# Cosine attention and an MLP mixer on one core: three row tiles of the sixth batch leave the slots and join the end's block products

## The chip, the core and the metric

One core of a Trainium2 chip runs the whole program. The metric is device time in microseconds (us) of one execution, as the median of the runs shown. The profile is of one other execution, whose span runs from its first to its last instruction. Engines are named as in the profile: PE (TensorE), DVE (VectorE), ACT (ScalarE), POOL (GpSimd), and SP, which here only issues DMAs. Each engine works through its own instructions in the order of the program, and waits where an operand or a buffer is not ready.

## The reference

```python
q, k, v: (8, 12, 448, 64)                      # batches, heads, rows, width; tau = 0.1
q_n = q / (norm(q) + 1e-6);  k_n = k / (norm(k) + 1e-6)
attn = softmax(q_n @ k_n.T / tau)
x = (attn @ v).transpose(0, 2, 1, 3).reshape(8, 448, 768)
h = relu(x.transpose(0, 2, 1) @ w_tok1) @ w_tok2      # 448 -> 256 -> 448, along the rows
u = x + h.transpose(0, 2, 1)
out = u + relu(u @ w_ch1) @ w_ch2                      # 768 -> 1536 -> 768, along the columns
```

Operands of the matrix products are fp16, sums and outputs fp32. In the code the hidden values `relu(u @ w_ch1)` are `gts`, and `u` is kept in `u16`, with its transpose in `ut`. The batches are numbered 0 to 7, so the sixth batch is number 5 in the code.

## The kernel before

**Slots.** A pair is two heads of one batch: 6 pairs to a batch, 48 in all. The loop at L920 runs one slot for each pair `i` from 7 to 47, and the program is written out by hand in the order in which each engine is to take it. A slot's own work is a software pipeline:

- PE: the scores of pair i (`score`, L345, three of them and the remainder, L352), weights times v for pair i-1 (`pv_rest`, `pv`, L367 and L384), and the token products of pairs i-2 (`tok2`, L434) and i-1 (`tok1`, L420).
- ACT: the exponentials (L346, L353), and the two steps of the norms of pair i+2 (L277, L278).
- DVE: the sums of squares of pair i+3 (L266, at the end of the slot), the last steps of the norms (L274, L275), and the evictions `rec`, `x`, `rt` and `u`.
- POOL, in `side(i)`: a cast of v of pair i (L228, and L230 in every third slot), the squares of pair i+3 (L250), and the scaling of k and q of pair i+2 into `kq` (L298, L306).
- SP: `tpose_dma(i + 2)` (L330) transposes that `kq` into `qk` by DMA, and the scores of slot i+2 read it. Behind it on the same queue come the loads of later pairs, the output stores, and `udma` (L443), which transposes `u`.

**Channel units.** The two channel products are cut into units: a G unit is one of 12 column tiles of `w_ch1` for a batch (`m_ch1`, 6 matmuls of 448 columns, L467), an F unit is one half of a row tile of the output (`m_ch2`, 12 matmuls of 384 columns, L483, with an addition of `u` on DVE and a store). They stand in `queue`. In each slot `fed[0]` grows by `fed[1]`. One unit is issued after `pv`, and more after `tok2` while `due()` says so. `refill(b)` queues a batch's units and sets `fed[1]` to their sum over six slots. A batch of 448 rows is three row tiles of 128 rows and one of 64, and the last 64 rows of an even batch share a tile (number 3 of the odd batch) with the first 64 of the next.

**The end.** Batches 6 and 7 (`B0`, `B1`) do not go through units. After the last slot their channel products are done as 2 by 2 block products with 7 block multiplications in place of 8 (the sums and differences of operands are made by `fast_weights1`, `fast_weights2`, `fast_x` and `fast_g`). The first channel product is `p1` to `p7` (L587). The second is `q1` to `q7` (`prod2`, L675): seven products of 6 matmuls of 384 columns for each pair of row tiles in `TILES`. Three pairs are done so, and the shared tile of batches 6 and 7 by plain matmuls (`shared_half`, L743). In their blocks the recorded line of DVE's and POOL's additions is that of the helper `tt`, L536, so the prediction names them by tile.

Weights for the block products are prepared inside the last slots. In POOL's order: `fast_weights2(1)` (`t1w`) in slot 41, ahead of that slot's scaling; `fast_weights2(2)` (`t2w`) in slots 45 and 46; `fast_weights1(1)` (`s1w`) after that; and `fast_weights1(4)` (`s4w`) after slot 47's cast. DVE makes `s2w` from `s1w` in slot 47, right after the evictions of `pv` of pair 46:

```python
            if i == NP_ALL - 2:
                fast_weights2(2, (1,))
                fast_weights1(1, nc.gpsimd)
```

PE's PSUM buffers with the tag "b" are two. In slot 47 and just after it they are used in turn by `psO` of pair 46 (two), `psU` of pair 45, `psR` of pair 46, and `psO` of pair 47 (two), so that PE's `pv_rest` of pair 47 waits until DVE has evicted `psR` of pair 46 (`rt`).

Of the kernel before, what the change touches and what calls it, by code (L numbers as in the profile page):

```python
# [22 lines left out]
def kernel(  # L23
# [12 lines left out]
    nc = tc.nc  # L36
# [479 lines left out]
    def ch2_units(b):  # L516
        cuts = ((0, DH, None), (DH, D, 0))
        ends = ((0, DH, None), (DH, D - 128, 0), (D - 128, D, D - 128))
        if b == B - 1:
            order = [(m, c) for m in (3, 0, 1, 2) for c in (ends if m == 2 else cuts)]  # L520
        elif b == 0:
            order = [(m, c) for c in cuts for m in range(3)]
        else:
            order = [(m, c) for m in range(3) for c in cuts]
            if b % 2:
                order[5:5] = [(3, cuts[0])]
                order.append((3, cuts[1]))
        return [(ns(hi - lo, CT), lambda wide, m=m, lo=lo, hi=hi, st=st: m_ch2(b, m, lo, hi, st, wide))
                for m, (lo, hi, st) in order]

    HD, HC = DT // 2, CT // 2
    B0, B1 = B - 2, B - 1
    fw = {}

    def tt(eng, out, a, b, op):
        eng.tensor_tensor(out=out, in0=a, in1=b, op=op)  # L536
# [4 lines left out]
    def tail_tiles():  # L541
        fw["t"] = {k: xtile(k, "x", [128, HD, S]) for k in (1, 2)}
        fw["e1"] = tail.tile([128, 2, S], FP32, name="e1_0", tag="e1")
        fw["s"] = [tail.tile([128, HD, C // 2], FP16, name=f"s{n}w1") for n in (1, 2, 4)]

    def xtile(k, name, shape):
        return (tail if k < 3 else tail2).tile(shape, FP16, name=f"t{k}{name}", tag=f"t{k}x", bufs=1)
# [47 lines left out]
    def gpart(i, b, d):  # L595
        return gts[B0 // 2][:, HC * i + 2 * d:HC * i + 2 * d + 2, b * S:(b + 1) * S]

# [28 lines left out]
    def p4(d):  # L626
        prod1(4, d, py, False)
        tt(nc.vector, gpart(1, 0, d), py[d][:, :, 0:S], e["e1", d][:], ALU.add)
# [21 lines left out]

    TILES = ((0, 1), (2, 6), (4, 5))
    ENDS = ((0, 256), (256, DH))
    sg, xo, yo, zo, eo, orow = {}, {}, {}, {}, {}, {}

    def gtile(t, i, j0=0, j1=HC):
        return gts[B0 // 2][:, HC * i + j0:HC * i + j1, 128 * t:128 * t + 128]

    def fast_g(g, k, j0=0, j1=HC):
        if k == 1 and j0 == 0:
            sg[g] = {n: tail2.tile([128, HC, 128], FP16, name=f"s{n}g_{g}", tag=f"s{n}g", bufs=1) if g == 1  # L660
                     else xtile(n, f"g_{g}", [128, HC, 128]) for n in (1, 2, 3, 4)}
        r1, r2 = TILES[g]
        s = sg[g]
        a, b, op = {1: (gtile(r2, 0, j0, j1), gtile(r2, 1, j0, j1), ALU.add),
                    2: (s[1][:, j0:j1], gtile(r1, 0, j0, j1), ALU.subtract),
                    3: (gtile(r1, 0, j0, j1), gtile(r2, 0, j0, j1), ALU.subtract),
                    4: (gtile(r1, 1, j0, j1), s[2][:, j0:j1], ALU.subtract)}[k]
        tt(nc.vector, s[k][:, j0:j1], a, b, op)

# [8 lines left out]
    def j3(ap):  # L678
        return ap.rearrange("p (j e) -> p j e", e=128)

    def urow(t, h):
        b, slot = (B0, t) if t < 3 else (B1, t - 3)
        return u16[b][:, HD * h:HD * (h + 1), slot]

    def etile2(kind, g, bufs=2):
        eo[kind, g] = tail2.tile([128, DH], FP32, name=f"{kind}_{g}", tag=kind.replace("f", "e") if kind in ("f5", "f16", "f167") else kind, bufs=bufs)
        return eo[kind, g][:]

# [7 lines left out]
    def f1u(g):  # L696
        tt(nc.gpsimd, j3(etile2("f1u", g, 1)), j3(eo["f1", g][:]), urow(TILES[g][1], 0), ALU.add)

    def q5(g):
        zo[g], yo[g] = [ps2.tile([128, 512], FP32, name=f"ps{a}o_{g}", tag="s") for a in "ZY"]  # L700
        prod2(5, g, zo[g], True)
        nc.scalar.activation(out=etile2("f5", g), in_=zo[g][:, 0:DH], func=AF.Copy)

    def q6(g):
        prod2(6, g, yo[g], True)
        tt(nc.vector, etile2("f16", g), yo[g][:, 0:DH], eo["f1", g][:], ALU.add)
        tt(nc.gpsimd, j3(eo["f16", g][:]), j3(eo["f16", g][:]), urow(TILES[g][0], 1), ALU.add)
        tt(nc.gpsimd, j3(eo["f5", g][:]), j3(eo["f5", g][:]), urow(TILES[g][1], 1), ALU.add)

# [7 lines left out]
    def q7(g):  # L717
        prod2(7, g, yo[g], False)
        tt(nc.vector, etile2("f167", g), yo[g][:, 0:DH], eo["f1", g][:], ALU.add)
        tt(nc.gpsimd, orow[g][1][:, DH:D], eo["f167", g][:], eo["f5", g][:], ALU.add)  # L720

    def store_row(t, o, lo=0, hi=D, first=nc.sync):
        b, m = (B0, t) if t < 3 else (B1, t - 4)
        r = 0
        for n, (c, p0, p1_) in enumerate(pieces(*MAIN[m])):
            eng = nc.sync if n else first
            eng.dma_start(out=out[b].rearrange("(p c) d -> c p d", c=NCH)[c, p0:p1_, lo:hi], in_=o[r:r + p1_ - p0, lo:hi])
            r += p1_ - p0

    def q3(g):  # L730
        prod2(3, g, zo[g], False)
        tt(nc.vector, orow[g][0][:, DH:D], zo[g][:, 0:DH], eo["f16", g][:], ALU.add)

    def q4(g):
        prod2(4, g, yo[g], False)
        tt(nc.vector, orow[g][1][:, 0:DH], yo[g][:, 0:DH], eo["f1u", g][:], ALU.add)
        store_row(TILES[g][1], orow[g][1])

    def shared_half(h):
        lo = DH * h  # L740
        psF = ps2.tile([128, 512], FP32, name=f"psF_shared_{h}", tag="s")
        for ct in range(CT):
            nc.tensor.matmul(psF[:, 0:DH], gts[B0 // 2][:, ct, 384:512], wc2t[:, ct, lo:lo + DH],  # L743
                             start=(ct == 0), stop=(ct == CT - 1))
        o = qkv.tile([128, DH], FP32, name=f"ost_shared_{h}", tag=("qf", "kf")[h])
        (c, p0, p1_), = pieces(384, S)
        for r, b, slot in ((0, B0, 3), (64, B1, 0)):
            tt(nc.vector, j3(o[r:r + 64]), j3(psF[r:r + 64, 0:DH]), u16[b][r:r + 64, HD * h:HD * (h + 1), slot], ALU.add)
        for r, b in ((0, B0), (64, B1)):
            nc.sync.dma_start(out=out[b].rearrange("(p c) d -> c p d", c=NCH)[c, p0:p1_, lo:lo + DH], in_=o[r:r + 64])  # L750

# [11 lines left out]

    KEPT = 6000.0

    def refill(b):
        new = ch1_units(b) + ch2_units(b)
        segs = NPAIR + 1 if b == 0 else NPAIR
        fed[1] = (sum(t for t, _ in new) - (KEPT if b == 0 else 0.0)) / segs
        queue.extend(new)  # L770

    with tc.manual_schedule():
# [147 lines left out]
        for i in range(NPAIR + 1, NP_ALL):  # L920
# [20 lines left out]
            elif pj == 2 and 1 < b < B - 1:  # L941
                refill(b - 1)
            side(i)
            if i == NP_ALL - NPAIR:
                fed[1] = (sum(t for t, _ in queue) - fed[0]) / NPAIR
# [17 lines left out]
            if i == NP_ALL - 3:  # L963
                early.close()
                tail = ctx.enter_context(tc.tile_pool(name="tail", bufs=1, side="right", reuse_waits="tile"))
                tail_tiles()
            if i == NP_ALL - 2:
                fast_weights2(2, (1,))
                fast_weights1(1, nc.gpsimd)
# [3 lines left out]
        while queue:  # L973
            unit(True)
        gts[B0 // 2] = mix.tile([128, CT, 2 * S], FP16, name=f"gt_{B0 // 2}", tag="gt", bufs=1)
        p1(0)
# [5 lines left out]
        for k in (3, 4):  # L982
            fw["t"][k] = xtile(k, "x", [128, HD, S])
        fast_weights1(3, nc.vector)
        p1(1)
# [33 lines left out]
        p6(2)  # L1019
        p4(0)  # L1020
        relu(1, 0, 0)
        p4(1)
        relu(1, 0, 1)
        p7(2)
        bank2("Z", 1)
        p5(1)
# [4 lines left out]
        p4(2)  # L1031
        relu(1, 0, 2)
        p3(1)
        fast_g(0, 1)
        fast_g(0, 2)
        p3(2)
        q1(0)
        f1u(0)
        relu(0, 1, 1)
        fast_g(0, 3)  # L1040
        q1(1)
        relu(1, 1, 1)
        q5(0)
        relu(0, 1, 2)
        relu(1, 1, 2)
        q6(0)
        fast_g(0, 4)
        for g in range(2):
            rows(g)
            q2(g)  # L1050
            fast_g(g + 1, 1)
            q7(g)
            fast_g(g + 1, 2)
            q3(g)
            store_row(TILES[g][0], orow[g][0])
            fast_g(g + 1, 3)
            q4(g)
            fast_g(g + 1, 4)
            if g == 0:
                f1u(1)  # L1060
            else:
                q1(2, ENDS)
                f1u(2)
            q5(g + 1)
            q6(g + 1)
        rows(2)
        q3(2)
        store_row(TILES[2][0], orow[2][0], DH, D)
        q7(2)
        shared_half(0)  # L1070
        q4(2)
        shared_half(1)
        for (lo, hi), eng in zip(ENDS, (nc.sync, nc.scalar)):
            q2(2, lo, hi)
            store_row(TILES[2][0], orow[2][0], lo, hi, eng)

# [34 lines left out]
```

## Time and profile before

| | |
|---|---|
| median of 3 runs | 383.1 us (382.84 to 383.28) |
| the profiled execution | 380.6 us, span 378.8 us |
| busy in the span | PE 366.2, POOL 286.9, DVE 246.0, ACT 234.0 us |
| granted TensorE clock | 1.00 |
| PE between 60 and 310 us | no idle time |
| last matmul starts its group at | 372.55 us |

The busy time of an engine is the union of its instructions. Matmuls overlap each other, so a group's own length is read from the start of one group to the start of the next: an F unit takes 1.95 us so, a G unit 1.135 us, a product of the second block stage 0.975 us.

### The profile page before, as it was taken

The numbers are of one execution on the slowest core, as the hardware profiler recorded it, in microseconds if no ns is written. First come the engines' busy times: TensorE is split into PE (matmuls) and PEld (weight loads), VectorE is DVE, ScalarE is ACT, GpSimd is POOL, SyncE is SP. The second block draws the span as 40 slices with busy tenths as digits, with TensorE's granted clock in tenths as the row PEclk, the third lists the DMA queues.
The fourth block names the chain that finished last, engine by engine and source line by source line (L and its number), as shares of the span: only waits on it lengthen the run. The fifth ranks groups of instructions, "written<-read, shape, count | busy, mean of one in ns | idle before, by whom it ended". The sixth has DMA issues, their size and how long they took to land.

```text
span 378.8 us, 10270 instructions
## 1 busy us (share of the span) xinstructions
PE 366.2 (97%) x4086; PEld 240.1 (63%) x4086; DVE 246.0 (65%) x559; ACT 234.0 (62%) x401; POOL 286.9 (76%) x414
## 2 busy tenths in 40 slices
PE   7788999999999999999999999999999999999994
PEld 6466666676567666667656666666666667655562
DVE  7789766777436574557444675456545776887963
ACT  5999887855666447855675466764677574426410
POOL 8999997979667577678657757767869987389760
PEclk9999999999999999999999999999999999999999
DMA  8999999989997898969895798977984874200144
GB/s 225 281 231 218 262 239 200 207 159 157 217 220 141 180 201 209 187 167 170 213 210 121 175 184 198 195 162 197 205 192 104 158 160 99 57 0 3 55 123 116
DMA packets 116256, 64.35 MB, mean 170 GB/s; under 512 B 72304, under 2 KB 112880, under 8 KB 116208
## 3 DMA queue, kind: packets, MB, share of 16 engines
q1 hardware_dynamic: 110208, 58.20, 69.9%
q0 software_dynamic: 5616, 5.21, 8.7%
q8 instruction: 32, 0.52, 0.6%
q10 hardware_dynamic: 384, 0.29, 0.2%
q14 instruction: 16, 0.13, 0.1%
HBM read 43.45 MB, written 11.01 MB: 144 GB/s over the span
## 4 chain that ended last, share of the span: by engine, by line
PE 81%; DMA 7%; DVE 4%; POOL 3%; ACT 1%; issue 1%; SPq 0%; DVEq 0%; POOLq 0%
PE psG L467 21%; PE psF L483 19%; PE psO L384 9%; PE psS L345 7%; PE psU L434 5%; PE psR L420 5%; DMA qf<-in_q_dram 3%; PE psY L587 3%; PE psYo L675 2%; DMA kf<-in_k_dram 2%; PE psX L587 2%; PE psQ L352 2%; POOL kq L298 2%; PE psZ L587 2%; PE psZo L675 1%; DVE ssq L266 1%
## 5 line engine op out<-in xcount | busy, mean ns | idle before, releaser
L346 ACT ACTIVATE pt<-psS 128x896 f16<-128x896 f32 (+1 forms) x156 | 132.7, 916 | 51.9 <-PE psS L345 51.9
L483 PE MATMUL psF<-wc2t,gt 128*128 128x384 f16 x504 | 88.4, 326 | 0.0
L467 PE MATMUL psG<-ut,wc1t 128*128 128x448 f16 x432 | 88.1, 352 | 0.0
L298 POOL TENSOR_TENSOR kq<-kf,rn 128x384 f16<-128x384 f32 (+1 forms) x47 | 41.9, 891 | 59.2 <-DVE rn L275 55.6
L483 PEld LDWEIGHTS <-gt 128*128 128x128 f16 x504 | 47.1, 98 | 27.8
L467 PEld LDWEIGHTS <-wc1t 128*128 128x128 f16 x432 | 40.2, 98 | 32.4
L470 ACT ACTIVATE gt<-psG 128x448 f16<-128x448 f32 x72 | 38.9, 540 | 33.1 <-PE psG L467 33.1
L266 DVE TENSOR_REDUCE ssq<-sq 128x15 f32<-128x960 f32 (+2 forms) x51 | 56.2, 1101 | 2.9 <-ACT sq L248 1.8
L423 DVE TENSOR_SCALAR rt<-psR 128x256 f16<-128x256 f32 x48 | 20.1, 418 | 50.8 <-PE psR L420 50.8
L298 POOL TENSOR_TENSOR kq<-qf,rn 112x512 f16<-112x512 f32 x45 | 47.0, 1045 | 3.0
L345 PE MATMUL psS<-qk 64*128 64x448 f16 x312 | 41.3, 355 | 3.5 <-DVE qk L324 2.8
L487 DVE TENSOR_TENSOR ost<-psF,u 128x384 f32<-128x384 f32 (+1 forms) x48 | 25.7, 536 | 26.8 <-PE psF L483 25.4
L250 POOL TENSOR_TENSOR sq<-qf 112x512 f32<-112x512 f32 x39 | 40.6, 1040 | 0.0
L250 POOL TENSOR_TENSOR sq<-kf 128x384 f32<-128x384 f32 (+1 forms) x46 | 40.2, 873 | 0.3 <-DMA kf<-in_k_dram 0.3
L384 PE MATMUL psO<-vt,pt 128*128 128x65 f16 (+1 forms) x1024 | 39.2, 193 | 0.0
L388 DVE TENSOR_TENSOR x<-psO,rec 128x256 f16<-128x256 f32 x82 | 34.8, 425 | 2.8
L384 PEld LDWEIGHTS <-pt 128*128 128x128 f16 (+1 forms) x1024 | 34.2, 97 | 3.5 <-issue 0.9
L437 DVE TENSOR_TENSOR u<-psU,x 128x512 f16<-128x512 f32 x48 | 32.3, 674 | 2.0 <-PE psU L434 0.5
L434 PEld LDWEIGHTS <-w2t 128*128 128x128 f16 x384 | 24.8, 98 | 7.9 <-issue 1.0
L420 PEld LDWEIGHTS <-w1t 128*128 128x128 f16 x384 | 24.8, 98 | 7.9 <-issue 2.1
L434 PE MATMUL psU<-rt,w2t 128*128 128x128 f16 x384 | 29.3, 219 | 0.5 <-POOL w2t L198 0.5
L420 PE MATMUL psR<-x,w1t 128*128 128x128 f16 x384 | 29.3, 219 | 0.2 <-DVE u L437 0.2
(128 smaller groups left out, 481.0 us busy)
## 6 DMA issues: line engine op xcount, KB each, us to landing
qf<-in_q_dram SPq DMA_DIRECT2D x47, 224.0 KB, 4.2
kf<-in_k_dram SPq DMA_DIRECT2D x36, 192.0 KB, 3.9
vf<-in_v_dram SPq DMA_DIRECT2D x36, 192.0 KB, 3.8
vf<-in_v_dram SPq DMA_DIRECT2D x12, 224.0 KB, 7.6
kf<-in_k_dram SPq DMA_DIRECT2D x11, 224.0 KB, 7.2
wc1t<-in_moe_w_ch_dram POOLq DMA_DIRECT2D x4, 576.0 KB, 10.1
wc2t<-in_moe_w_ch_dram POOLq DMA_DIRECT2D x2, 1152.0 KB, 11.8
out_dram<-ost SPq DMA_DIRECT2D x6, 336.0 KB, 3.6
```

Of the source, the lines that this page charges most:

```text
L250: nc.gpsimd.tensor_mul(out=dst, in0=src, in1=src)
L266: nc.vector.tensor_reduce(out=st["ssq"][0:n, sl], in_=st["sq"][0:n, sl], axis=AXX.X, op=ALU.add)
L298: eng.tensor_tensor(out=kq[0:p, a, 0:n].rearrange("p c g e -> p g c e"), in0=st["kq"[a]][:].rearrange("p (g c) e -> p g c e", g=2), in1=_b ...
L345: nc.tensor.matmul(psS[:, hh, 0:S], qk[hb, c * n:c * n + 128], qm[hb], start=True, stop=True)
L346: nc.scalar.activation(out=pts[i % 2][0:n, 2 * S * c:2 * S * (c + 1)].rearrange("p (h s) -> p h s", h=2), in_=psS[0:n, :, 0:S], func=AF.Ex ...
L384: nc.tensor.matmul(psO[:, m, 0:E + 1], pts[i % 2][0:n, at:at + 128], vt[0:n, i % HP, nch * hh + c, 0:E + 1], start=(old(i) and c == 0), st ...
L388: nc.vector.tensor_tensor(out=st["x"][:, :, hh * E:(hh + 1) * E], in0=psO[:, :, 0:E], in1=_bcast_free(rec[:], E), op=ALU.mult)
L420: nc.tensor.matmul(psR[:, tt], w1t[:, w1[m], tt * 128:(tt + 1) * 128], st["x"][:, m], start=(m == 0), stop=(m == 3))
L434: nc.tensor.matmul(psU[:, m], w2t[:, tt, lo:lo + 128], st["rt"][:, tt], start=(tt == 0), stop=(tt == TT - 1))
L467: nc.tensor.matmul(psG[:, 0:S], wc1t[:, dt, ct * 128:(ct + 1) * 128], ut[b][:, dt].rearrange("p m s -> p (m s)")[:, lo:lo + S], start=(dt ...
L470: nc.scalar.activation(out=gt[:, ct, (b % 2) * S:(b % 2 + 1) * S], in_=psG[:, 0:S], func=AF.Relu)
L483: nc.tensor.matmul(psF[:, 0:hi - lo], gt[:, ct, at:at + 128], wc2t[:, ct, lo:hi], start=(ct == 0), stop=(ct == CT - 1))
```

## The change

Three row tiles of batch 5 (`KEPT_B` in the diff; its tiles 0, 1 and 2; six F units) are no longer issued as units. Only the tile that batches 4 and 5 share remains (two F units, in slots 46 and 47). The end's second channel product works on ten row tiles in five pairs (`n` in the diff), where it had six in three pairs and one by plain matmuls: tiles 7, 8 and 9 are those of batch 5, and tile 3 is the shared one of batches 6 and 7. `shared_half` is gone. Batch 5's hidden values stay in their buffer, and batch 6's are written beside them, in the place of batch 4's. Batch 7's go into a new tile, with two small DMAs that bring batch 6's last 64 rows beside them (`g_shared`) and one for `u` (`u_shared`). The first pair's operands are made in part in slot 46: two `fast_g` on DVE, at the slot's end. The feed of channel work is no longer set anew at each `refill`, but is 4350 from slot 14 and 3400 from slot 38. From slot 42 it is, as before, a sixth of what is left.

Where the units land, in slots 36 to 47 (F b.m is tile m of batch b, a and b its halves; the bar is where the second place in the slot begins):

| slot | before | after |
|---|---|---|
| 36 | G4.10, G4.11, F4.0a | G4.5 to G4.8 |
| 37 | F4.0b, F4.1a | G4.9 to G4.11, F4.0a |
| 38 | F4.1b, F4.2a | F4.0b |
| 39 | F4.2b, G5.0 to G5.2 | F4.1a, F4.1b |
| 40 | G5.3 to G5.7 | F4.2a, F4.2b |
| 41 | G5.8 to G5.11 | G5.0 to G5.2 |
| 42 | F5.0a | G5.3, G5.4 |
| 43 | F5.0b, F5.1a | G5.5, G5.6 |
| 44 | F5.1b | G5.7, G5.8 |
| 45 | F5.2a | G5.9, G5.10 |
| 46 | F5.3a, F5.2b | G5.11, F5.3a |
| 47 | F5.3b | F5.3b |

```diff
     def ch2_units(b):
...
+            if b == KEPT_B:
+                order = [(3, c) for c in cuts]
...
-    TILES = ((0, 1), (2, 6), (4, 5))
+    TILES = ((7, 8), (0, 1), (2, 9), (4, 5), (6, 3))
...
+    RATES = {2 * NPAIR + 2: 4350.0, NP_ALL - 10: 3400.0}
     def refill(b):
         new = ch1_units(b) + ch2_units(b)
-        segs = NPAIR + 1 if b == 0 else NPAIR
-        fed[1] = (sum(t for t, _ in new) - (KEPT if b == 0 else 0.0)) / segs
+        if b == 0:
+            fed[1] = (sum(t for t, _ in new) - KEPT) / (NPAIR + 1)
         queue.extend(new)
...
             side(i)
+            fed[1] = RATES.get(i, fed[1])
             if i == NP_ALL - NPAIR:
                 fed[1] = (sum(t for t, _ in queue) - fed[0]) / NPAIR
...
             if i == NP_ALL - 2:
+                fast_g(0, 1)
+                fast_g(0, 2)
                 fast_weights2(2, (1,))
                 fast_weights1(1, nc.gpsimd)
...
         p7(2)
+        fast_g(0, 3)
+        fast_g(0, 4)
         bank2("Z", 1)
...
-        rows(2)
-        q3(2)
-        store_row(TILES[2][0], orow[2][0], DH, D)
-        q7(2)
-        shared_half(0)
-        q4(2)
-        shared_half(1)
-        for (lo, hi), eng in zip(ENDS, (nc.sync, nc.scalar)):
-            q2(2, lo, hi)
-            store_row(TILES[2][0], orow[2][0], lo, hi, eng)
+        g = n - 1
+        q6(g)
+        q5(g)
+        f5u(g)
+        rows(g)
+        q7(g)
+        q3(g)
+        store_row(TILES[g][0], orow[g][0], DH, D)
+        q4(g)
+        for (lo, hi), eng in zip(ENDS, (nc.scalar, nc.sync)):
+            q2(g, lo, hi)
+            store_row(TILES[g][0], orow[g][0], lo, hi, eng)
```

## The prediction

> **What bounds the kernel now.** I read the page's busy times first, then the windows, the chain that ended last, and the timelines of POOL, DVE and PE from slot 40 on.
>
> ```profile
> PE 366.2 (97%) x4086; PEld 240.1 (63%) x4086; DVE 246.0 (65%) x559; ACT 234.0 (62%) x401; POOL 286.9 (76%) x414
> ```
> ```profile
> 180.00:220.00 40.00, 40.00 (x427) 25.78 (x426) 21.21 (x54) 24.51 (x45) 25.83 (x42) 1.00 0.81 182
> 290.00:300.00 10.00, 10.00 (x124) 6.92 (x124) 7.34 (x19) 6.48 (x12) 9.65 (x17) 1.00 0.83 168
> ```
>
> PE is the bound over the whole run: busy 97%. But the windows (columns PE, PEld, DVE, ACT, POOL, clock) show that POOL's room is not everywhere: 14 us idle of 40 in the middle, 0.35 of 10 at 290. The chain says the same: for 20 us it leaves PE.
>
> ```profile
> 289.18 0.69 PE psS L345 x6
> ...
> 290.69 2.04 POOL sq L250 x3
> ...
> 303.72 0.83 POOL kq L298
> 305.58 0.75 issue
> 306.41 3.84 DMA qk<-kq
> 310.29 0.74 PE psS L345 x6
> ```
>
> So in the last slots PE already meets POOL's pace: the scores at 310.29 waited for the transpose of a `kq` begun 6.57 us earlier. The same step in slots 41 to 43 is 287.30 to 293.79, 6.49 at most. The transposes' median landing is 3.3 us, which would make it 6.05.
>
> ```profile
> 277.40 0.83 POOL L298 TENSOR_TENSOR kq<-kf,rn 128x384 f16<-128x384 f32 x1 [2.95 <-DVE rn L275]
> ...
> 282.50 4.84 POOL L536 TENSOR_TENSOR t1w<-wc2t 128x768 f16<-128x768 f16 x3
> 287.30 0.83 POOL L298 TENSOR_TENSOR kq<-kf,rn 128x384 f16<-128x384 f32 x1
> ...
> 292.69 0.83 POOL L298 TENSOR_TENSOR kq<-kf,rn 128x384 f16<-128x384 f32 x1
> ...
> 297.80 0.82 POOL L298 TENSOR_TENSOR kq<-kf,rn 128x384 f16<-128x384 f32 x1
> ...
> 303.72 0.83 POOL L298 TENSOR_TENSOR kq<-kf,rn 128x384 f16<-128x384 f32 x1 [0.78 <-DVE rn L275]
> ...
> 313.35 4.54 POOL L536 TENSOR_TENSOR s1w<-wc1t 128x2304 f16<-128x2304 f16 x1
> ```
>
> From 277.40, in slot 40, POOL has no idle but 0.78 until `s1w` ends at 317.83. A slot costs POOL 5.11 us (292.69 to 297.80), 5.39 with the extra cast (287.30 to 292.69), and `t1w` adds 4.80 in slot 41. A slot's own PE work is 2.73 (289.11 to 293.79, less one F of 1.95).
>
> **PE's work.** Six F units leave the slots: 6 x 1.95 = 11.70. At the end `shared_half` goes (2 x 1.95 = 3.90), and two pairs come, 14 products x 0.975 = 13.65: +9.75. Net -1.95 if PE stays the bound.
>
> **The feed up to slot 40.** Slots 14 to 37 are 5.81 us or longer in the new order, more than POOL's 5.39, so PE stays dense and moved units cost nothing; the cover is POOL's idle of 1.2 to 2.9 us per slot. When slot 40 begins, two F and three G fewer are done: 3.90 + 3.41 = 7.31 earlier, less 0.14, since slot 38 has one unit only (`pv_rest` took 0.43 for 0.30 after such a slot): 7.17. Slot 40 begins at 273.43 - 7.17 = 266.26.
>
> **Slots 40 to 47: POOL becomes the bound.** POOL's scaling in slot 40 cannot move ahead: its operand comes 3.97 us after the slot's first scores (273.43 to 277.40), through three exponentials on ACT. From there POOL's work is the same as before, without the 0.78: `s1w` ends at 317.83 - 7.17 - 0.78 = 309.88, 7.95 earlier. PE alone would be faster: slot 40 takes 6.63, slot 41 with three G 6.13, slots 42 to 45 with two G 5.00 each, slot 46 5.81, so slot 47 would start at 304.83, 12.1 earlier. It can't: pair 43's `kq` starts at 270.23 + 9.90 = 280.13 and its scores come 6.05 to 6.57 later, at 286.2 to 286.7, where PE is ready at 284.0. That is a stall of 2.2 to 2.7 at the head of slot 43, then 0.4, 0.1 and 0.1 (POOL's 5.39, 5.11, 5.11 against 5.00). Behind the waiting scores all of PE's queue stands still, and POOL's loads and casts are not what it waits for. On SP's queue `tpose_dma` comes up to 1 us late in slots 39 and 40 (the same issues in shorter slots); both scores have more than 1 us to spare. Slot 47 starts at 307.6 to 308.1. ACT, which gets two evictions of G in each of slots 42 to 45 (0.54 each) beside exponentials and norms of 3.6, has 4.7 of 5.0 and stays under the pace of POOL.
>
> **Two `fast_g` on DVE at the head of slot 47.** These rows price them:
>
> ```profile
> 319.43 1.35 DVE L536 TENSOR_TENSOR s2w<-s1w,wc1t 128x2304 f16<-128x2304 f16 x1
> ...
> 322.47 0.41 DVE L423 TENSOR_SCALAR rt<-psR 128x256 f16<-128x256 f32 x1
> ...
> 349.53 2.32 DVE L536 TENSOR_TENSOR t2g<-t1g,gt 128x768 f16<-128x768 f16 x1
> ...
> 357.02 0.89 DVE L536 TENSOR_TENSOR s3g<-gt 128x768 f16<-128x768 f16 x1
> ```
> ```profile
> 346.99 4.44 POOL L536 TENSOR_TENSOR gt<-e,e 128x896 f16<-128x896 f32 x2
> ...
> 356.29 1.19 POOL L536 TENSOR_TENSOR orow<-f,f 128x384 f32<-128x384 f32 x1
> ```
>
> A `fast_g` takes 0.54 alone. The two here end at 351.85 and 357.91, each 0.42 after POOL's instruction ended (351.43, 357.48): DVE's sum of two SBUF operands waits for the POOL instruction that runs. In the new order they come up at about 308.0, while `s1w` runs until 309.88. The first ends at 310.3, the second at 310.8 to 311.2 (the higher if POOL's cast, 0.51, gets in between). Queued behind them on DVE are `x` of pair 46 (1.15), `s2w`, an F eviction, `u` and `rt` of pair 46. `x` ends at 312.0 to 312.35, 2.1 to 2.5 after `s1w`; before it ended at 319.43, 1.60 after it. From `x` to the end of `rt` it is 3.45 as before, and `pv_rest` of pair 47 waits for that `rt`:
>
> ```profile
> 322.76 0.46 PE L367 MATMUL psO<-vt,pt 64*128 64x65 f16 x8
> ```
>
> Its `rt` ended at 322.88, so this wait is already the last one there. It moves by -7.95 + 0.5 to 0.9 = -7.45 to -7.05. So 11.70 us of PE work taken out bring 7.25.
>
> The Trainium skill, page "SBUF — State Buffer", section "Who interferes with whom", states an exclusive lock between DVE and GpSimd for the whole of an instruction, given to whoever issues first. By it alone the cast may win or lose, so the two ends above would stand, and `rec` and `x`, which read one SBUF operand at most, would not be blocked.
>
> The same skill, page "TensorE: Matmul & The Clock Gate", "Part 1: The HAM clock gate", halves PE's clock after an idle window of about 3.4 us. The trace shows 1.00 in all windows from 60 us, with no gap so long to test it; by the rule a stall of 2.7 stays below, and a halved window would add an estimated 1.7 us.
>
> **The end.** Up to the second product nothing moves: `fast_g(0, 3)` and `(0, 4)` fall into DVE's idle 2.24 before 346.47, and even blocked by `t4w` (1.6 each) they end 1.6 late, just ahead of the PSUM buffers that `q5` and `q6` want. The stall of 0.28 at 351.63 (`t2g`) goes, since the first pair's operands are ready. The pairs run at 6.83 each; DVE has some 5.5 there (four `fast_g` at 0.75, five additions at 0.5), POOL 4.5. The new transfers cost nothing: `g_shared` and `u_shared` are issued while SP is empty (nothing between 324 and 357) and read by the last pair, over 20 us later; uncovered they would cost a landing, 2 to 3 us. The held tiles' stores move to the end with their pairs, 4 to 5 issues of 0.56 on SP in 6.83. At the last store, SP issues two DMAs where it issued three behind each other, and DVE no longer has two `ost_shared` additions ahead:
>
> ```profile
> 372.55 1.15 PE L675 MATMUL psXo<-wc2t,gt 128*128 128x256 f16 x12
> 374.55 1.70 SPq L727 DMA_DIRECT2D out_dram<-orow  x3
> ```
>
> The last issue ended 2.55 after the last matmul (373.70); now about 2.0: -0.55, with 0 and -1.1 as ends.
>
> **Sum.** -7.25 + 9.75 - 0.28 - 0.55 = +1.7, against the profiled span: 378.8 becomes 380.5, the execution 380.6 becomes 382.3. The median shown is 2.5 above that execution, so I add the difference: 384.8. With the ends: +0.9 to +2.4, that is 384.0 to 385.5.
>
> **Rivals.**
>
> *PE stays the bound (faster).* If POOL's scalings run earlier than I think, slot 47 starts 12.1 earlier; the two `fast_g` add 1.1 ahead of `rt`: -11.0 + 8.92 = -2.1, 381.0. For it: POOL idles a quarter of the whole run. Against it: POOL's unbroken rows from 277.40. It decides if slot 43's scores don't wait.
>
> *DVE isn't held by `s1w` (no change).* Then the `fast_g` end at 309.1, `x` at 310.5, 8.9 earlier: -8.9 + 8.9 = 0, 383.1. Against it: the rows above.
>
> *The five pairs don't run dense (slower still).* If DVE, with a POOL instruction in each gap, needs 7.4 a pair in place of 6.83, four pairs add 2.3: 387.1. For it: DVE is 94% busy from 350 to 360. Against it: PE stays gapless there from 352.
>
> **How the numbers follow.** Forecast 0.62, PE-bound 0.13, no lock 0.12, loose pairs 0.13. A measurement of this kernel can tell about 0.2% from no change, 0.77 us. Faster: the PE-bound case and a little of the second, 0.16. Same: the second and the forecast's low edge, 0.14. Slower: 0.70. The range leaves out most of the first rival and half of the last: 382.3 to 386.6.
>
> **What would show it.** Right: PE idle of 2 us or more before L345's scores near 284 to 287, released by the transposed `qk`; POOL without idle from slot 40 to `s1w`; a DVE `s1g` of about 2 us beside `s1w`; `pv_rest` of pair 47 waiting for `rt`; no gap in the five pairs. Wrong: PE dense through slots 41 to 47, or gaps among the products of L695.

## The result, and the profile after

The changed kernel takes 385.62 us (median of 6 runs, 385.19 to 386.94); the kernel before, now with six runs, 382.15 us (380.34 to 383.28). The ratio is 1.0104, with a 95% interval of 1.0069 to 1.0140: slower by 3.5 us, inside the range, where the prediction's own sum was +1.7. Its level, 384.8, lies closer than its difference because it was added to a median of 383.1, of three runs, and the runs that came later were faster. That closeness is luck.

The profiled execution of the changed kernel took 386.94 us, with a span of 385.1 (before: 380.6 and 378.8). The page says that PE has almost the same work and a smaller share, and that POOL and DVE are busier:

```profile
PE 365.8 (95%) x4074; PEld 239.1 (62%) x4074; DVE 254.8 (66%) x567; ACT 234.8 (61%) x405; POOL 296.1 (77%) x422
```

The windows (length, PE, PEld, DVE, ACT, POOL, granted clock, share of DMA, GB/s) show where: PE was full from 290 to 300 before, and now it isn't, beside a POOL that is as full as it was.

```profile
10.00:20.00 10.00, 7.33 (x76) 4.79 (x78) 7.84 (x15) 7.50 (x13) 8.82 (x10) 0.66 1.16 285
290.00:300.00 10.00, 9.27 (x124) 6.19 (x121) 6.42 (x17) 8.16 (x15) 9.65 (x16) 1.00 0.74 163
```

The first of these lines is in code that both kernels share: the clock was 0.66 there and 1.00 before, and slot 15 begins at 92.65 instead of 90.50. In the profiles below that start lies anywhere from 90.5 to 95.7 (93.1 in the other profile of the kernel before, in "before, relieved"), so I compare lengths from slot 15's first scores on. The table cuts each profiled span at four places: the first scores (L345) of slots 15 and 40, the end of `rt` of pair 46, and PE's end.

| kernel | start to 15 | 15 to 40 | 40 to rt(46) | to PE's end | to span's end | time, us |
|---|---|---|---|---|---|---|
| before | 90.50 | 182.93 | 49.45 | 50.82 | 5.1 | 382.15 |
| prediction for after | 90.50 | 175.76 | 49.37 | 60.29 | 4.55 | 384.8 |
| after | 92.65 | 177.15 | 49.34 | 59.96 | 6.0 | 385.62 |

Of the 6.3 us by which the two spans differ, 2.15 are the start. The rest is +4.15: -5.78 up to slot 40, -0.11 to `rt` of pair 46, +9.14 to PE's end, +0.9 behind it. Two of these terms are not the predicted ones: 1.39 are missing up to slot 40, and the end is 1.45 worse.

In slots 40 to 47 the length came out to 0.03 us, and the waits did not lie where they were put. PE's timeline (start, us, group; in brackets the idle time ahead and what ended it):

```profile
283.75 0.74 PE L345 MATMUL psS<-qk 64*128 64x448 f16 x6 [0.87 <-DMA qk<-kq]
289.62 0.74 PE L345 MATMUL psS<-qk 64*128 64x448 f16 x6 [0.70 <-DMA qk<-kq]
295.52 0.74 PE L345 MATMUL psS<-qk 64*128 64x448 f16 x6 [0.73 <-DMA qk<-kq]
313.20 0.74 PE L345 MATMUL psS<-qk 64*128 64x448 f16 x6 [1.59 <-DMA qk<-kq]
```

These are slots 42, 43, 44 and 47, where one stall of 2.2 to 2.7 was forecast for slot 43. POOL's timeline is the forecast one: `kq` of slot 40 starts 3.96 after the slot's scores (forecast 3.97), and `s1w` ends 39.6 later (forecast 39.65).

```profile
273.76 0.83 POOL L298 TENSOR_TENSOR kq<-kf,rn 128x384 f16<-128x384 f32 x1 [0.93 <-DVE rn L275]
278.86 4.83 POOL L536 TENSOR_TENSOR t1w<-wc2t 128x768 f16<-128x768 f16 x3
...
308.85 4.54 POOL L536 TENSOR_TENSOR s1w<-wc1t 128x2304 f16<-128x2304 f16 x1
```

What the prediction had not looked at enough is SP's queue:

```profile
277.21 1.22 SPq L443 DMA_TRANSPOSE ut<-u  x1
278.53 0.98 SPq L502 DMA_DIRECT2D out_dram<-ost  x2
279.62 1.28 SPq L330 DMA_TRANSPOSE qk<-kq  x1
...
301.92 1.23 SPq L330 DMA_TRANSPOSE qk<-kq  x1
308.61 1.19 SPq L443 DMA_TRANSPOSE ut<-u  x1
309.89 1.26 SPq L330 DMA_TRANSPOSE qk<-kq  x1
```

Two things are to be read in it. The transpose issued at 279.62 has its `kq` ready at 276.36, 2.60 after POOL began it: it is 3.3 late, because loads, a transpose of `u` and a store stand ahead of it without a gap (k's load among them took 1.17, where it took 0.45 in the kernel before). It also landed later: 4.1 after its issue, where the same one took 3.1 in the kernel before. And from 303.15 to 308.61 SP does nothing: the head of its queue is the first transpose into `ut` of batch 7. That buffer was batch 5's, and the last G unit of batch 5, which reads it, is now in slot 46 (it ends at 308.58). The scores' transpose of pair 47 stands behind it, although its `kq` was ready 3.0 earlier. So slot 47 starts with the wait of 1.59.

DVE at the head of slot 47; then DVE at the head of slot 21; then PE there:

```profile
312.81 1.00 DVE L536 TENSOR_TENSOR s1g<-gt 128x768 f16<-128x768 f16 x1
...
318.73 0.41 DVE L423 TENSOR_SCALAR rt<-psR 128x256 f16<-128x256 f32 x1
```
```profile
136.02 1.12 DVE L487 TENSOR_TENSOR ost<-psF,u 64x384 f32<-64x384 f32 x2 [1.39 <-PE psF L483]
137.17 0.42 DVE L423 TENSOR_SCALAR rt<-psR 128x256 f16<-128x256 f32 x1
```
```profile
137.65 0.28 PE L367 MATMUL psO<-vt,pt 64*128 64x65 f16 x7 [0.25 <-DVE rt L423]
```

`s1g` ended 0.42 after `s1w`, as the rows of before said it would. It took 1.00 and not the forecast 2, because it came up only 0.58 before the end of `s1w`. The second and third fences show where the 1.39 went: in slots 20 and 21 the last unit is now half of a shared tile, whose eviction is two additions of 64 rows (1.12 us) where a full tile's is one (0.56). `rt`, which frees a PSUM buffer for the next slot's `pv_rest`, stands behind it.

### The profile page after: what moved, and what is told of

It reads as the page before. It is cut to its first block, busy times and chain, and to the rows that moved or that the text cites. A ratio compares the mean times of both kernels' runs of the same rounds, so it can differ in the third digit from the quotient of the medians.

```text
span 385.1 us, 10276 instructions
## 1 busy us (share of the span) xinstructions
PE 365.8 (95%) x4074; PEld 239.1 (62%) x4074; DVE 254.8 (66%) x567; ACT 234.8 (61%) x405; POOL 296.1 (77%) x422
## 4 chain that ended last, share of the span: by engine, by line
PE 80%; POOL 6%; ACT 5%; DVE 4%; DMA 2%; issue 1%; SPq 0%; ACTq 0%; POOLq 0%; DVEq 0%
PE psG L467 19%; PE psF L483 17%; PE psO L384 9%; PE psS L345 7%; PE psU L434 5%; PE psR L420 4%; PE psYo L695 4%; ACT pt L346 3%; PE psY L590 3%; PE psZo L695 3%; PE psXo L695 2%; PE psX L590 2%; PE psZ L590 2%; DMA qk<-kq 2%; PE psQ L352 2%
## 5 line engine op out<-in xcount | busy, mean ns | idle before, releaser
L467 PE MATMUL psG<-ut,wc1t 128*128 128x448 f16 x432 | 89.5, 352 | 0.0
L483 PE MATMUL psF<-wc2t,gt 128*128 128x384 f16 x432 | 75.6, 326 | 0.0
L483 PEld LDWEIGHTS <-gt 128*128 128x128 f16 x432 | 40.5, 98 | 24.1
L345 PE MATMUL psS<-qk 64*128 64x448 f16 x312 | 41.9, 358 | 7.8 <-DMA qk<-kq 3.9
L487 DVE TENSOR_TENSOR ost<-psF,u 128x384 f32<-128x384 f32 (+1 forms) x42 | 22.6, 539 | 27.0 <-PE psF L483 26.9
```

The source lines that it names most:

```text
L345: nc.tensor.matmul(psS[:, hh, 0:S], qk[hb, c * n:c * n + 128], qm[hb], start=True, stop=True)
L467: nc.tensor.matmul(psG[:, 0:S], wc1t[:, dt, ct * 128:(ct + 1) * 128], ut[b][:, dt].rearrange("p m s -> p (m s)")[:, lo:lo + S], start=(dt ...
L483: nc.tensor.matmul(psF[:, 0:hi - lo], gt[:, ct, at:at + 128], wc2t[:, ct, lo:hi], start=(ct == 0), stop=(ct == CT - 1))
```

## The experiments

Two theories stood against each other. One: from slot 40 POOL's chain sets the pace, as predicted, and the feed costs 1.39 for a reason of its own. The other: POOL only looks busy, and SP's queue or the feed is what costs. Lengths are read from one profile each, times are medians. Between slot 40 and `rt` of pair 46 the runs e6 and e8 have the same code as the changed kernel, and show 49.45 and 49.81 where it shows 49.34; e11 and e12 share their code too, with 46.69 and 47.47. The landings of the DMAs differ by that much (the transpose that slot 43 waits for took 5.1 in e11 and 5.9 in e12), so a difference under 0.8 in this column says little by itself.

| kernel | 15 to 40 | 40 to rt(46) | to PE's end | to span's end | time (runs) | ratio to before |
|---|---|---|---|---|---|---|
| e1 t1w early | 177.16 | 49.05 | 59.97 | 5.9 | 386.30 (6) | 1.0077 to 1.0130 |
| e2 ut behind | 177.16 | 49.22 | 59.97 | 5.6 | 385.78 (6) | 1.0077 to 1.0119 |
| e3 both | 177.15 | 48.27 | 59.97 | 5.9 | 384.60 (6) | 1.0050 to 1.0091 |
| e4 old feed | 179.66 | 49.29 | 59.96 | 6.0 | 388.90 (6) | 1.0152 to 1.0204 |
| e6 batch 1 order | 175.72 | 49.45 | 59.97 | 6.0 | 386.33 (1) | |
| e8 end's queue | 177.15 | 49.81 | 59.97 | 5.4 | 389.83 (1) | |
| e9 e3, loads on ACT | 177.14 | 48.98 | 59.97 | 5.9 | 386.82 (4) | 1.0116 to 1.0192 |
| e10 loads on ACT alone | 177.14 | 52.13 | 59.97 | 5.8 | 389.22 (1) | |
| e11 e3, q and k on ACT | 177.15 | 46.69 | 59.98 | 5.7 | 383.92 (10) | 1.0008 to 1.0063 |
| before, relieved | 182.93 | 49.39 | 50.85 | 5.0 | 382.09 (10) | 0.9965 to 1.0014 |
| e12 all | 175.74 | 47.47 | 59.96 | 5.9 | 382.09 (12) | 0.9985 to 1.0028 |
| e13 no fast_g | 177.14 | 48.39 | 60.47 | 6.0 | 386.14 (1) | |

### POOL's weight work out of slot 41

```diff
-            if i == NP_ALL - 7:
-                fast_weights2(1)
+            if NP_ALL - 13 <= i < NP_ALL - 10:
+                fast_weights2(1, (i - NP_ALL + 13,))
```

> The changed kernel with t1w's three subtractions (1.6 us each on POOL) taken from slot 41 and made one each in slots 35, 36 and 37, where POOL idles 1.8 to 2.1 us per slot. PE's work and order are the same. From slot 40's first scores to the end of rt of pair 46 the changed kernel took 49.34 us, with PE idle for 4.06 of it; the kernel before 49.45, PE idle for 0.14. Theory (POOL's chain sets the pace from slot 40): s1w ends 4.8 us earlier, the waits ahead of the scores of slots 42, 43 and 44 go, and what is left is the wait of slot 47's scores behind the first transpose of batch 7's ut on SP's queue: the stretch falls to 47.0 to 47.8, the time by 1.5 to 2.3 from 385.6, to 383.3 to 384.1. Rival A (PE alone would set it): the stretch falls to 45.3, the time by 4. Rival B (POOL is beside the path, SP's queue makes the waits): nothing, 385.6.

Measured: 49.05, where the changed kernel has 49.34, and no gain in time. `s1w` ends 0.7 earlier against slot 40, not 4.8. Rival B comes nearest. POOL is no longer without idle, and PE waits as before (slots 42 and 43, and 1.56 ahead of slot 47):

```profile
280.58 0.83 POOL L298 TENSOR_TENSOR kq<-kf,rn 128x384 f16<-128x384 f32 x1 [1.85 <-DVE rn L275]
```
```profile
283.68 0.74 PE L345 MATMUL psS<-qk 64*128 64x448 f16 x6 [0.85 <-DMA qk<-kq]
289.81 0.74 PE L345 MATMUL psS<-qk 64*128 64x448 f16 x6 [0.97 <-DMA qk<-kq]
```

POOL's `kq` now waits 1.85 for `rn`, which comes from PE's scores through ACT and DVE. So POOL follows PE, and something between `kq` and the scores holds PE. The chain of POOL's work was long enough to explain the length, and it was not alone.

### Batch 7's first ut transpose behind the scores' transpose

```diff
+            if i == NP_ALL - 3:
+                udma(NP_ALL - 6)
             if i > NPAIR + 1:
-                tok2(i - 2)
+                tok2(i - 2, pe=(i == NP_ALL - 4))
```

> The changed kernel with the first transpose into batch 7's ut (it waits until the last G unit of batch 5 in slot 46 has read the buffer) issued on SP behind the scores' transpose of pair 47 instead of ahead of it; nothing else moves. In the changed kernel the scores of slot 47 waited 1.59 us, and their transpose was issued 3.0 us after its kq was ready. Theory (POOL's s1w and the two fast_g beside it set rt of pair 46): the 1.59 go, slot 47 starts 1.5 earlier, but x of pair 46 still ends 2.4 after s1w, so the stretch from slot 40 to rt of pair 46 stays at 49.0 to 49.4 and the time at 385.3 to 385.6. Rival (the wait of slot 47 is what sets the path): the stretch is 47.7 to 47.9, the time 384.0.

Measured: the wait of slot 47 is gone, the length is 49.22, and the time 385.78, 0.2 over the forecast. The theory's length holds: with this wait gone, the two `fast_g` beside `s1w`, which ends at 311.76, end as late against slot 40 as they did with it (`s2g` at 312.95 and `x` right behind it).

```profile
310.80 1.38 DVE L536 TENSOR_TENSOR s1g<-gt 128x768 f16<-128x768 f16 x1
```

> Both together: t1w early and batch 7's first ut transpose behind the scores' transpose of pair 47. Theory (two bounds one behind the other, POOL's chain first, the ut transpose second): the gain is larger than the sum of the two alone. The stretch from slot 40 to rt of pair 46 falls from 49.34 to 45.8 to 46.8, near PE's own 45.28, and the time by 2.6 to 3.5, to 382.1 to 383.0. Rival (the two are independent, their gains add up): if the ut transpose alone brings nothing, this is what t1w early brings, 383.3 to 384.1.

Measured: 48.27 and 384.60. More than the two alone (0.29 and 0.12 become 1.07, and the time is 1.0 below the changed kernel's), as bounds in a row would give, but little over the scatter of 0.8, short of 45.8 to 46.8, and the time is outside both forecasts. The scores of slots 42 and 43 still wait 1.00 and 0.95, with no `t1w` ahead of them. SP's queue in slots 40 and 41 of this kernel:

```profile
278.01 1.27 SPq L330 DMA_TRANSPOSE qk<-kq  x1
...
281.04 1.19 SPq L443 DMA_TRANSPOSE ut<-u  x1
282.33 0.99 SPq L502 DMA_DIRECT2D out_dram<-ost  x2
283.43 1.46 SPq L330 DMA_TRANSPOSE qk<-kq  x1
```

From one scores' transpose to the next SP issues for 5.4 us; the loads of q, k and v stand where lines are left out, with gaps of 0.1 only. That is a third bound beside POOL's 5.4 per slot.

### SP's queue relieved

The edit is that of e3, and in `load_qk`, for q, k and `kr`:

```diff
     def load_qk(i):
+        eng = nc.scalar if i >= NP_ALL - 4 else nc.sync
...
-        nc.sync.dma_start(out=st["q"][:]...
+        eng.dma_start(out=st["q"][:]...
```

> The kernel of the run with both edits (t1w early, batch 7's first ut transpose behind the scores' transpose), and the loads of q and k of the last four pairs issued by ACT instead of SP (1.0 us of issue in slots 38 to 41, 2.3 where kr comes with them). In the run with both edits SP's queue had no idle from the transpose of slot 39 to 286, and the scores of slots 42 and 43 still waited 1.00 and 0.95 us although POOL had no t1w there. Theory (behind POOL's chain the next bound is SP's queue, which holds the scores' transposes back by 1.8 to 3.3 us): both waits go or fall under 0.3, and the stretch from slot 40's first scores to rt of pair 46 falls from 48.27 to 46.2 to 47.3, the time by 1 to 2, to 382.6 to 383.6. Rival (what is left is the latency from scores through the exponentials, norms and scalings to the scores two slots on): the waits stay within 0.3 of what they were, the time too.

Measured: 48.98, the opposite of the forecast, by one stall that no theory had:

```profile
269.34 2.17 ACTq L130 DMA_DIRECT2D kr<-in_k_dram  x2
271.56 0.54 ACT L354 ACTIVATE pt<-psQ 128x448 f16<-128x448 f32 x1 [5.88 <-POOL sq L251]
```

`kr`'s load waited 2.9 (ACT's queue had issued k's by 266.47), and on ACT the exponentials stand behind it. PE lost 2.71 in slot 40. After that no scores waited for a transpose. The expectation of the run with q's and k's loads on ACT, below, says that this load waited for its buffer. The record does not show that: by the code, the scaling of pair 35, in slot 33, was the last to read that buffer. The chain of work gives another cause, the landing of earlier loads of v:

```profile
266.85 4.02 DMA vr<-in_v_dram
...
270.88 0.63 ACTq L130
```

The second of the load's two issues comes 0.02 after the landing of the rest of v, and the first, at 269.34, comes 0.1 after the landing of the load of v that was issued at 265.55 and took 3.7. No run tests why they wait for it.

The same edit without those of e3:

> The changed kernel with only the loads of q and k of the last four pairs moved from SP to ACT; t1w stays in slot 41. Theory (POOL's chain is the first bound, SP's queue the second, so lifting the second alone brings nothing): the wait of slot 42 (0.87) falls, kq of pair 43 still starts 13.8 to 13.9 us after slot 40's first scores, slot 43's scores come 5.4 to 6.0 after it, s1w ends 43.3 to 43.6 after slot 40's first scores, and the stretch stays at 48.9 to 49.4. Rival (SP's queue alone is the bound and POOL's chain only follows it): the stretch falls to 48.0 or less.

Measured: 52.13, which answers nothing about SP, since the same stall is in it (3.05) and costs more than its length (see the last section). So `kr` went back to SP (`load_rest` without `eng`), with e3's edits again:

> As the run with the last loads of q and k on ACT, t1w early and batch 7's first ut transpose behind the scores' transpose, but kr stays on SP. In that run the scores of slots 42 to 47 no longer waited for a transpose, but ACT stood 2.9 us behind kr's load of slot 39, which waited for its buffer, and the scores of slot 40 lost 2.71 by it: 48.98 us from slot 40's first scores to rt of pair 46. Theory (SP's queue was the second bound, and only kr's wait hid the gain): no stall of 1 us or more in slot 40, the waits of slots 42 and 43 under 0.5, the stretch at 46.0 to 47.2, the time 2.1 to 3.3 below the 385.6 of the changed kernel, 382.3 to 383.5. Rival (any load on ACT delays the exponentials by as much as it frees SP): the stretch stays at 48.0 or more.

Measured: 46.69, and 383.92 us: inside the theory's range for the length, and 0.4 over it for the time. Slot 43 still waits 0.51, the others don't. PE is busy for 45.51 of the 46.69. The three reliefs together give 2.65 of the length, where each of the first two alone gave 0.3 or less. The run with everything together has the same code in this stretch and shows 47.47, a gain of 1.9.

In the kernel before, `t1w` early and the loads of q and k on ACT:

> The kernel before the change with the same reliefs where they exist there: t1w in slots 35 to 37 instead of 41, the loads of q and k of the last four pairs on ACT. (The first ut transpose did not wait there.) In the kernel before PE idled only 0.14 of the 49.45 us from slot 40's first scores to rt of pair 46. Theory (there PE is the bound, and the queues became the bound only when the change took PE's work away): the stretch stays at 49.2 to 49.6 and the time within 0.5 us of that of the kernel before. Rival (POOL and SP held that kernel back too): 48.5 or less, and 1 us or more faster.

Measured: 49.39 and a ratio of 0.9965 to 1.0014. The median is 0.9 below that of the kernel before in the same session, more than the 0.5 forecast, but the interval allows no change, and the stretch shows none. The same relief does nothing there for the kernel before, where PE is the bound in this stretch. The queues came forward because the change took PE's work away there.

### The feed

> The changed kernel with the feed of before: every batch's units spread evenly over the slots up to the next refill, no rates reset by slot. Slots 14 to 37 get back the order of before; then F4.1b comes in slot 38, F4.2 in 39, two, three, two, one, two and two G in slots 40 to 45, F5.3 in 46 and 47. Theory (slots 40 to 47 take what POOL needs, whatever PE has to do): slots 14 to 37 are 1.44 us shorter, but slot 40 starts only 3.3 earlier against slot 14 than in the kernel before, where the changed kernel had 5.8 (7.2 without the 1.44); slot 40 to rt of pair 46 stays at 49.0 to 49.6; the time rises by 2.3 to 2.7 from 385.6, to 387.9 to 388.3. Rival (the reset feed is what costs, POOL does not bind): the 1.44 come back, 384.2.

```diff
-        if b == 0:
-            fed[1] = (sum(t for t, _ in new) - KEPT) / (NPAIR + 1)
+        segs = NPAIR + 1 if b == 0 else NPAIR
+        fed[1] = (sum(t for t, _ in new) - (KEPT if b == 0 else 0.0)) / segs
...
-            fed[1] = RATES.get(i, fed[1])
```

Measured: slot 40 begins 179.66 after slot 15, 3.27 earlier than in the kernel before; the length from there is 49.29; the time 388.90. The theory holds to 0.05 us by the profile; the time is 0.6 over its range. The stretch does take its 49.3 whatever PE has to do, and the earlier feed is what the change lives on.

> The changed kernel with the F units of batch 1 in another order: the shared tile's first half before the third tile's first half, its second half before the third tile's second half. So neither of its halves is the last unit of slots 20 and 21, where the two additions of 64 rows (1.12 us on DVE where a full tile takes 0.56) stood ahead of rt. Theory: slots 21 and 22 lose 0.7 us each, slot 14's first scores to slot 40's go from 183.93 to 182.4 to 182.7 (189.71 minus 7.2), and all behind it moves with them. Rival (the 1.44 come from the moved slot borders as such): 183.6 to 184.

```diff
+            elif b == 1:
+                order = [(m, cuts[h]) for m, h in ((0, 0), (0, 1), (1, 0), (1, 1), (3, 0), (2, 0), (3, 1), (2, 1))]
             elif b % 2:
```

Measured: 175.72 from slot 15 to 40, which is 7.21 less than before and 1.43 less than in the changed kernel; the forecast was 7.17. No wait for `rt` is left in slots 21 and 22. This settles the missing 1.39: it is the order of two units. (The single time, 386.33, contains a start of 93.35.)

### The lock

```diff
             if i == NP_ALL - 2:
-                fast_g(0, 1)
-                fast_g(0, 2)
...
         p4(0)
+        fast_g(0, 1)
...
         relu(1, 0, 1)
+        fast_g(0, 2)
```

> The run with batch 7's first ut transpose behind the scores' transpose, and with it the two fast_g on DVE moved from the head of slot 47 into the tail (after p4(0) and after relu(1,0,1)). In that run x of pair 46 ended 2.29 us after s1w and rt of pair 46 followed 3.37 later through s2w, an F eviction and u on DVE; PE waited 1.02 for it. Theory (with the ut wait gone, the two fast_g beside s1w set rt): x ends 1.4 to 1.7 after s1w, the stretch from slot 40's first scores to rt of pair 46 falls from 49.22 to 48.2 to 48.7, and the tail stays at 59.9 to 60.2. Rival (POOL's s1w alone, through s2w, sets rt whatever is ahead of x): the stretch stays at 49.1 to 49.3.

Measured: `x` ends 1.46 after `s1w` instead of 2.29, and the length falls from 49.22 to 48.39, by 0.83. The tail takes 0.5 more, since the two `fast_g` now stand there. So the two `fast_g` ahead of `x` cost what was forecast, 0.5 to 0.9. That alone is not the lock, since the edit takes their own work on DVE away too. What shows the lock is the length of `s1g`: 1.38 in e2, 1.00 in the changed kernel and 0.58 in e1, where it came up 0.96, 0.58 and 0.16 before the end of `s1w`. Each time it ends 0.42 after `s1w`.

### The end

```diff
-        store_row(TILES[g][0], orow[g][0], DH, D)
+        store_row(TILES[g][0], orow[g][0], DH, D, nc.scalar)
```

> The changed kernel with the store of the last pair's first half row (two issues) on ACT's queue instead of SP's. In the changed kernel SP issued the last six stores back to back in 4.01 us, from 1.28 before PE's end to 2.73 after it, and the span ended 6.0 after PE's end (5.1 in the kernel before). Theory (SP's issues set the end): the last issue ends 1.3 earlier, and the span ends 4.9 to 5.5 after PE's end. Rival (the bytes of the last rows set it: 393 KB and 192 KB more are in flight at PE's end): 5.8 to 6.2.

Measured: 5.4, which would fit the theory, but its mechanism is not there: SP's last four issues take 3.03 us from 0.33 ahead of PE's end, as they do in the changed kernel (3.04 from 0.31 ahead). With the same edit in e12 the end is 5.9. Nothing is settled by it.

### All together

> All four edits that gave something in the profiles, together, on the changed kernel: t1w early, batch 7's first ut transpose behind the scores' transpose, the last loads of q and k on ACT (kr on SP), batch 1's units in the order that keeps the shared tile's halves from the end of slots 20 and 21, and the store of the last pair's first half row on ACT. Theory (they lie at different places of one chain, so they add up): slot 15's first scores to slot 40's 175.7 us, from there to rt of pair 46 46.5 to 47.0, from there to PE's end 59.9 to 60.1, then 5.2 to 5.6 to the span's end; the time 1.7 to 2.2 below the 383.9 of the run with the first three, 381.7 to 382.2, which is the kernel before within what can be measured. Rival (what is saved early comes back as a wait on POOL or SP later): 383.5 or more.

Measured: 382.09 us, a ratio of 1.0006 (0.9985 to 1.0028): the kernel before, within what can be measured. The first and third pieces are as expected. The stretch is 47.47, not 47.0 or less, since slot 43 waited 1.24, and the end stays at 5.9, not 5.6 or less. So the time fell into its range although two of the four pieces did not. No version here beats the kernel before.

## Why the prediction was right or wrong

**The order of the terms was right.** Taking PE's work out of slots whose pace others set brings only what those others allow, and the end pays for every product: -5.9 and +9.1 in the profile. PE's five pairs ran without a gap at 6.83 each, so the rival of loose pairs falls. PE idles 4.06 in slots 40 to 47, so the rival of PE as the bound falls; e11 shows that it would have come near, at 46.69 instead of 45.28. The rival without a lock falls by the lengths of `s1g` (under "The lock").

**"Moved units cost nothing" failed.** The step looked at POOL's room and not at what a moved unit does to the slot that it ends. The feed's new order put a shared half last in slots 20 and 21, and its double addition held `rt`. It cost 1.39; e6 gives back 1.43.

**The stretch from slot 40 was right in size and too simple in cause.** Forecast 49.37, measured 49.34, by POOL's chain as forecast. That it fits to 0.03 is luck, with a scatter of up to 0.8 between profiles of the same code. PE's stall of 2.2 to 2.7 in slot 43 was not there: four waits of 0.70 to 1.59 were. And e1 takes 4.8 us of POOL's work away and gains 0.29. Four things stood there at nearly the same time: POOL's chain, SP's issues, the ut buffer's wait, and the two `fast_g` beside `s1w`. Removing one or two of them gave 0.1 to 1.1, removing three gave 2.65 and 1.87 (e11 and e12). "SP up to 1 us late" was the mis-sized step: it was 3.3 late in slot 40. How much of that wait is issue and how much the later landing, the runs do not separate. The wait of `udma` on the last G unit of batch 5 was missed altogether. Its 1.59 cost next to nothing, since the lock stood behind it (e2).

**The lock** was sized rightly: `x` ended 2.38 after `s1w`, where 2.1 to 2.5 was forecast. The Trainium skill, page "SBUF — State Buffer", section "Who interferes with whom", says that a DVE instruction with two SBUF inputs contends with a GpSimd instruction that reads SBUF. The 0.42 by which `s1g` outlasts `s1w`, whatever its own start, agrees with it.

**The end** was wrong in sign: -0.55 forecast, +0.9 measured. The step counted SP's last issues alone. Just ahead of them SP now has the two stores of the shared tile, of 192 KB each, where it had two of 96 KB, and from these stores on it took 3.04 (2.92 before). The last issue ended 2.73 after PE's end (2.55 before), and the last small stores took 3.1 to 3.9 to land where they took 1.8 to 2.5. That the larger stores ahead hold them back is likely, and no run here shows it.

**The tail** came out 0.33 shorter than forecast (59.96 against 60.29). The term for the stall that goes was too small. It was read as 0.28 of idle time, but in the kernel before, the product that starts at 350.49 is followed by the next only at 351.91, 1.42 later and not 0.975, and the one at 354.84 by the next 1.12 later. That is 0.45 and 0.15, 0.6 in all, and after the change the products of this stage start 0.99 or less apart.

Past the start, the profiles differ by 4.15: the forecast 1.7, +1.39 for the feed, +1.45 for the end, -0.33 for the tail, and 0.03 less in slots 40 to 47. The medians' 3.5 has an interval of 2.6 to 5.4, which holds that. The start's 2.15 is no part of the change.

## What to carry to other kernels

When work is taken off the bounding engine in one stretch, lay out every in-order queue there, the DMA queue's issues included, and add up each one's work per step: if several of them come within a few per cent, none of them alone is "the" bound, and relieving one may show nothing until the others are relieved too. Moving work to another slot also changes which instruction stands last ahead of the slot's critical eviction. A transfer that is moved to another engine's queue can wait there, and whatever stands behind it on that engine pays.

## What the runs showed of the hardware

PE's clock fell behind a stall of 3.05 us in slot 40, and not behind one of 2.71. A window of the run with the loads of q, k and `kr` on ACT alone, behind the gap that ended at 272.94 (the column with 0.64 is the clock):

```profile
273.00:276.00 3.00, 3.00 (x41) 2.12 (x41) 1.40 (x5) 2.72 (x5) 0.00 (x0) 0.64 0.99 226
```

An F unit (12 matmuls) there took 3.36 us instead of 2.11. From slot 40 to 41 that kernel took 11.48, where e8, with the same units, took 6.72: 3.05 of stall and 1.7 of clock. In the run with the gap of 2.71 (e9) the clock stays at 1.00 in these slots. The Trainium skill, page "TensorE: Matmul & The Clock Gate", "Part 1: The HAM clock gate", gives an idle window of about 3.4 us before the clock is halved. The traces differ: 3.05 was enough here, and in the first 20 us of the changed kernel, where PE has several gaps, the longest is 1.87, and the clock is 0.50 from 12 to 18 us:

```profile
11.84 0.55 PE L322 MATMUL pst<-id,kq 112*128 112x112 f16 x4 [1.87 <-DVE kq L298]
```

So the length of one gap does not decide it by itself, and what does, these runs do not show. The 1.7 is what the prediction had estimated for one halved window.
